# A decode kernel on one Trainium2 core: the last 64 rows of three weight matrices as two transfers each

## The chip, the core and the metric

The kernel runs on one core of one Trainium2 chip. TensorE (PE) multiplies matrices, VectorE (DVE), ScalarE (ACT) and GpSimd (POOL) do the rest, and SyncE (SP) issues nearly all loads, in one queue. A load is carried out by the core's 16 DMA engines. The metric is device time in microseconds of one launch.

## The reference

Two rounds of attention over a cache and a gated FFN, for four tokens (one per sequence) of 448 values:

```python
def _A_ref(x, k_cache, v_cache, wq, wo):          # 16 query heads, 8 KV heads of 256
    W = min(4096, max(256, Sk // 4))              # the last 2048 of 8192 positions
    q = (x @ wq).reshape(B, Sq, Hq, Dh) ...
    scores = jnp.einsum("bhqd,bhkd->bhqk", q, k) * (Dh ** -0.5)
    p = _softmax(scores, axis=-1)
    o = jnp.einsum("bhqk,bhkd->bhqd", p, v)
    return o ... @ wo

def _B_ref(x, w_gate, w_up, w_down):              # 448 -> 1792 -> 448
    return (_silu(x @ w_gate) * (x @ w_up)) @ w_down

x = x + _A_ref(_layernorm(x), ...)
x = x + _B_ref(_layernorm(x), ...)
x = x + _A_ref(_layernorm(x), ...)
x = x + _B_ref(_layernorm(x), ...)
return x
```

wq is 448 x 4096, gate and up are 448 x 1792, all bfloat16. Both rounds use the same weights and the same cache.

## The kernel before

The program is written as a graph of operations (`Graph.op`, and `Graph.dma` for loads). The order on each engine is written out by hand in the lists `SEQ_PE`, `SEQ_DVE`, `SEQ_ACT`, `SEQ_POOL` and `SEQ_SP`; `schedule` follows them and `_place_waits` puts semaphore waits only where an order does not give them already. So an engine never takes a later operation ahead of one that waits.

The cache goes through 27 buffers of 512 KB (`half`), and seven more that hold wq until the first queries have been made. `SLOTS` names the buffer of each load. A K load is 1 MB (L837) or 512 KB (L843), a V load 512 KB (L859). Each waits on SP, where it must, for the TensorE work that last used its buffer, and everything behind it in the SP queue waits too. VectorE transposes the K halves in place (L849); TensorE makes the scores (L883), transposes them (L930) and multiplies with V (L961); the results go through wo (L1014, L1006).

Weights are loaded once, by `load` (L487). With 448 = 3 x 128 + 64 rows, wq, gate and up come as three chunks of 128 rows and a tail of 64 rows. A tail is laid over all 128 partitions: the left half of its columns in partitions 0 to 63, the right half in partitions 64 to 127. In the source's access pattern the first dimension is the half (2), then the row (64), then the column:

```python
load(1 << 19, wq_sb[:, 3 * 4096:], A_wq[384:448, :].rearrange("r (h c) -> h r c", h=2), "wq3", 4096)
```

TensorE uses the tail of wq in `qproj` (L581, with `xe` as the small operand), those of gate and up in `ffn` (L706) and `ffn_row` (L643). In the SP queue the wq tail is the eighth load, behind three K loads, x and the three other chunks of wq. Between it and the tail of up stand seventeen loads, between that and the tail of gate nine; the large parts of gate, up and down come last of the weights.

The list `SEQ_PE` also has matrix products that compute nothing (L1093, "fillers": a zero operand is added to bank A); they stand at fixed places in the order.

Of the kernel before, what the change touches and what calls it, by code (L numbers as in the profile page):

```python
# [17 lines left out]
FF = 1792  # L18
# [140 lines left out]
class Op:  # L159
# [3 lines left out]
    def __init__(self, i, eng, kind, emit):  # L163
        self.i, self.eng, self.kind, self.emit = i, eng, kind, emit
        self.deps = {}
        self.nbytes = 0
        self.dsem = None
        self.dval = 0
        self.cells = self.rel = self.bank = ()
        self.inc = False  # L170
        self.val = 0
        self.waits = []


class Graph:
# [14 lines left out]
    def op(self, eng, kind, emit, r=(), w=(), bank=(), acc=()):  # L190
        o = Op(len(self.ops), eng, kind, emit)
        o.bank, o.tag = bank, self.tag
        self.ops.append(o)
        for k in r:
            d = self.writer.get(k)
            if d is not None:
                self._dep(o, d, d.eng != eng or eng != PE)
        for k in tuple(w) + tuple(acc):
            for d in self.readers.get(k, ()):
                self._dep(o, d, d.eng != eng or eng != PE)  # L200
            d = self.writer.get(k)
            if d is not None:
                self._dep(o, d, d.eng != eng or eng != PE)
        if eng != PE and "A" in bank:
            self._dep(o, self.last_a, self.last_a is not None and (self.last_a.eng != eng or eng != PE))
            self.last_a = o
        for b in bank:
            owner, now, before = self.banks.get(b, (eng, [], []))
            if owner != eng:
                owner, now, before = eng, [], now  # L210
            for d in before:
                self._dep(o, d, True)
            self.banks[b] = (owner, now + [o], before)
        for k in r:
            self.readers.setdefault(k, []).append(o)
        for k in tuple(w) + tuple(acc):
            self.writer[k] = o
            self.readers[k] = []
        return o

    def dma(self, nbytes, emit, sem, r=(), w=(), cells=(), run=4096):
        o = self.op(SP, "ld", emit, r=r, w=w)
        o.nbytes, o.cells, o.run = nbytes, cells, run
        if not cells:
            self._count(o, sem)
        return o

    def _count(self, o, sem):
        o.dsem = sem
        self.dcount[sem] = self.dcount.get(sem, 0) + 16  # L230
        o.dval = self.dcount[sem]

    def schedule(self, filler):
# [82 lines left out]
    def emit(self, eng_name, eng, sems, dsems):  # L316
        for o in self.order[eng_name]:
            for d in o.waits:
                if d.dsem is not None:
                    eng.wait_ge(dsems[d.dsem], d.dval)  # L320
                else:
                    eng.wait_ge(sems[d.eng], d.val)
            ins = o.emit(eng)
            if o.dsem is not None:
                ins.then_inc(dsems[o.dsem], 16)
            elif o.inc:
                ins.then_inc(sems[eng_name], 1)

# [10 lines left out]
def build(nc, A_x, A_k_cache, A_v_cache, A_wq, A_wo, B_x, B_w_gate, B_w_up, B_w_down, out):  # L339
    s0 = A_k_cache.shape[2] - WIN  # L340
    g = Graph()

    with ExitStack() as es:
# [8 lines left out]
        wq_sb = kv[:, NPOOL * HALF:]  # L352
# [75 lines left out]
        for a in range(4):  # L428
            g.op(DVE, "d1", lambda e, a=a: e.memset(qmask[32 * a:32 * a + 32, a:a + 1], DH ** -0.25), r=("qmask",),
                 w=(f"qmask{a}",))  # L430
# [10 lines left out]
        for P in range(2):  # L441
            g.op(DVE, "d1", lambda e, P=P: e.tensor_reduce(
                nmask[:, 2 * P:2 * P + 2], idq[:, P, :, 0:4, :].rearrange("p h a n -> p n h a"), AX.XY, ALU.add),
                r=("identb",), w=("rs0",))
        g.op(DVE, "d1", lambda e: e.tensor_reduce(negm[0][:, 0:1], nmask[:, :], AX.X, ALU.add), r=("rs0",), w=("negm0",))
        g.op(DVE, "d1", lambda e: e.tensor_scalar(negm[0][:, 1:2], negm[0][:, 0:1], -2.0, 1.0, op0=ALU.mult, op1=ALU.add),
             r=("negm0",), w=("negm0",))
# [10 lines left out]
        for h in range(2):  # L458
            for y in range(2):
                g.op(DVE, "d1", lambda e, h=h, y=y: e.tensor_copy(sel1[h][:, :, :, y, :], ivq[:, :, h:4:2, :]),  # L460
                     r=("identb",), w=(f"sel1{h}{y}",))
# [10 lines left out]
        for P in range(2):  # L472
            g.op(DVE, "d1", lambda e, P=P: e.tensor_reduce(
                osel[:, 2 * P:2 * P + 2], iv[:, :, 0, P, :, :].rearrange("p j y n -> p n j y"), AX.XY, ALU.max, negate=True),
                r=("identb",), w=("osel",))
        il = identb[:, :].rearrange("p (k y n) -> p k y n", y=2, n=2)
        g.op(DVE, "d1", lambda e: e.tensor_reduce(lomask[:, :], il[:, :, 1, :], AX.XY, ALU.add), r=("identb",),
             w=("lomask",))
# [3 lines left out]
        nw = [0]  # L482

        def load(nbytes, dst, src, key, run):
            nw[0] += 1
            g.tag = ("w", nw[0])
            g.dma(nbytes, lambda e: e.dma_start(dst, src), f"w{nw[0]}", w=key if isinstance(key, tuple) else (key,), run=run)  # L487
            g.tag = None

        load(4000, xio[0:B, :], A_x[:, 0, :], xio_k, 896)  # L490
        for cc in range(3):
            load(1 << 20, wq_sb[:, 4096 * cc:4096 * (cc + 1)], A_wq[128 * cc:128 * cc + 128, :], f"wq{cc}", 8192)
        load(1 << 19, wq_sb[:, 3 * 4096:], A_wq[384:448, :].rearrange("r (h c) -> h r c", h=2), "wq3", 4096)
        wo_v = A_wo.rearrange("(k p) n -> p k n", p=128)

        def load_wo(kvh):
# [3 lines left out]
        def load_ffn():  # L500
            for nm, wsb, src in (("wg", wg_sb, B_w_gate), ("wu", wu_sb, B_w_up)):
                load(3 * 458752, wsb[:, 0:3 * FF].rearrange("p (c n) -> p c n", c=3),
                     src[0:384, :].rearrange("(c p) n -> p c n", p=128), nm + "a", 3584)
                load(229376, wsb[:, 3 * FF:], src[384:448, :].rearrange("r (h c) -> h r c", h=2), nm + "b", 1792)
            load(1605632, wd_sb[:, :, :], B_w_down.rearrange("(c p) n -> p c n", p=128), "wd", 896)


# [283 lines left out]
        def x_in(e):  # L791
            clear(e, Zb[0:64, 12:16], 4)
            for cc in range(4):
# [6 lines left out]
             r=("z",), w=tuple(f"xs{t}" for t in range(B)) + tuple(f"x{t}" for t in range(B)), bank=("Z",))  # L800
# [197 lines left out]
        def out_proj(oi, ts, kvh, column):  # L998
# [21 lines left out]
            else:  # L1020
                g.op(PE, "opr", row, r=ro, acc=tuple(f"row{t}" for t in ts), bank=("A",))

        load_ffn()
        g.tag = None
        used = [None, None]
        gi, oc, waiting, wo_in = 0, 0, [], []
        for si, (heads, splits) in enumerate(zip(plan(), plan_splits())):
            where = {}
            for batch, split in zip(heads, splits):
                members, outs = [], []  # L1030
                for m in batch:
# [3 lines left out]
                    if kvh not in where:  # L1035
                        ts = sorted(t_ for b in heads for t_, _, k_ in b if k_ == kvh)
                        where[kvh] = (oc % 2, ts)
                        if used[oc % 2] != ts:
# [3 lines left out]
                                 w=tuple(f"oT{oc % 2}_{t_}" for t_ in range(B)))  # L1042
# [56 lines left out]
        dsems = {d: es.enter_context(nc.semaphore(f"d_{d}")) for d in g.dcount}  # L1099
# [28 lines left out]
def bass_interleave_layers__sliding_block_cached__swiglu_ffn__decode_kernel(  # L1128
    nc, A_x, A_k_cache, A_v_cache, A_wq, A_wo, B_x, B_w_gate, B_w_up, B_w_down, out
):  # L1130
    build(nc, A_x, A_k_cache, A_v_cache, A_wq, A_wo, B_x, B_w_gate, B_w_up, B_w_down, out)
# [28 lines left out]
```

## Time and profile before

| | |
|---|---|
| median of 3 runs | 313.45 us (311.82 to 316.13) |
| the profiled execution | 311.48 us, of which span 309.5 us |
| busy share: PE, DVE, ACT, POOL | 81%, 62%, 20%, 26% |
| loaded from HBM | 103.91 MB, 336 GB/s over the span |
| chain that ended last, by engine | PE 38%, DMA 23%, DVE 17%, SP's queue 15% |

The profile is of one execution. Times in its rows are from the start of the span. A row of the timeline gives start, duration, engine, line, operation, tiles and count, and in brackets how long the engine had been idle and what ended that. "SPq" is the SP queue issuing a load: its duration is how long the queue stood on that issue, not how long the load took. A row of the list of issues gives the load, the count, the size and the median time from issue to landing, in us. A row of the waits gives who waited for whom, the total in us, how often, and the longest.

### The profile page before, as it was taken

How to read it: one execution, taken by the hardware profiler on the slowest of the kernel's cores; microseconds unless marked ns; L12 is line 12 of the kernel's file. 1: busy time of each engine (PE TensorE's matmuls, PEld its weight loads, DVE VectorE, ACT ScalarE, POOL GpSimd, SP SyncE). 2: the span in 40 equal slices, each digit the busy share in tenths (PEclk: the TensorE clock that was granted, in tenths of full speed). 3: DMA queues.
4: the chain of work that ended last, by engine and by line, in shares of the span. 5: the costliest groups of instructions: out<-in, count | busy, mean ns of one | idle time of the engine just before them, and what ended most of it. 6: DMA issues, size and time to landing. Idle time of an engine off the chain costs nothing.

```text
span 309.5 us, 10634 instructions
## 1 busy us (share of the span) xinstructions
PE 249.5 (81%) x4683; PEld 140.9 (46%) x4683; DVE 193.2 (62%) x571; ACT 62.7 (20%) x173; POOL 80.3 (26%) x225
## 2 busy tenths in 40 slices
PE   4870478994759998778989788897999789989886
PEld 1320133431315754444545444363475437666565
DVE  4680085415235227886795959879479878768851
ACT  0001001010011132222223213223322332042311
POOL 0060012100201223404141442324223333233241
PEclk9977599998679999989999999999999999997997
DMA  7999995396999979999999999999999997999600
GB/s 295 428 313 280 358 411 238 142 327 251 315 399 364 318 267 329 420 411 412 330 346 411 411 413 413 411 381 340 374 420 412 408 407 284 367 421 406 277 2 5
DMA packets 26851, 104.60 MB, mean 338 GB/s; under 512 B 2609, under 2 KB 6709, under 8 KB 22837
## 3 DMA queue, kind: packets, MB, share of 16 engines
q1 hardware_dynamic: 26797, 103.92, 88.1%
q8 instruction: 37, 0.61, 0.8%
q14 instruction: 9, 0.07, 0.1%
q10 hardware_dynamic: 8, 0.00, 0.0%
HBM read 103.91 MB, written 0.00 MB: 336 GB/s over the span
## 4 chain that ended last, share of the span: by engine, by line
PE 38%; DMA 23%; DVE 17%; SPq 15%; issue 3%; ACT 3%; POOL 1%; DVEq 0%; ACTq 0%
DMA half<-in_A_v_cache_dram 14%; SPq L859 10%; PE A L1093 9%; DVE half L849 9%; PE S L883 6%; PE Y L961 6%; DMA half<-in_A_k_cache_dram 4%; DMA wo_sb<-in_A_wo_dram 4%; SPq L837 3%; PE A L1006 2%; PE Z L706 2%; PE A L1014 2%; DVE po L978 2%; SPq L487 2%; PE Y L930 2%
## 5 line engine op out<-in xcount | busy, mean ns | idle before, releaser
L849 DVE STREAM_TRANSPOSE half<-half 128x1024 uint32<-128x1024 uint32 x88 | 107.0, 1229 | 27.4 <-DMA half<-in_A_k_cache_dram 27.2
L1093 PE MATMUL A<-identb,small 128*128 128x512 bf16 x270 | 82.6, 403 | 5.0 <-DVE A L420 4.5
L961 PE MATMUL Y<-half,pT 128*8 128x256 bf16 (+1 forms) x1024 | 45.7, 280 | 9.8 <-DMA half<-in_A_v_cache_dram 7.1
L974 POOL TENSOR_TENSOR small<-small 128x2 f32<-128x2 f32 (+1 forms) x48 | 38.6, 807 | 36.8 <-DVE small L952 33.7
L883 PE MATMUL S<-half,qe 128*8 128x128 bf16 (+1 forms) x1536 | 44.7, 245 | 2.5 <-POOL qe L889 1.2
L1093 PEld LDWEIGHTS A<-identb,small 128*128 128x128 bf16 x270 | 24.2, 104 | 31.4 <-issue 14.6
L889 POOL TENSOR_TENSOR qe<-qc,tiny 128x64 bf16<-128x64 bf16 x64 | 18.1, 294 | 76.0 <-PE S L883 35.4
L883 PEld LDWEIGHTS S<-half,qe 128*8 128x8 bf16 x1536 | 31.2, 86 | 12.3 <-POOL qe L889 2.7
L978 DVE SCALAR_TENSOR_TENSOR po<-po,small,Y 128x256 bf16<-128x256 bf16 x48 | 22.6, 471 | 17.7 <-ACT po L976 17.4
L917 ACT ACTIVATE po<-S,small 104x128 bf16<-104x128 f32 (+1 forms) x48 | 19.3, 402 | 70.5 <-DVE small L913 70.3
L961 PEld LDWEIGHTS Y<-half,pT 128*8 128x8 bf16 (+1 forms) x1024 | 19.6, 84 | 23.2 <-DMA half<-in_A_v_cache_dram 8.6
L976 ACT ACTIVATE po<-Y 128x256 bf16<-128x256 f32 x48 | 18.4, 383 | 50.1 <-PE Y L961 33.2
L939 ACT ACTIVATE pT<-Y 128x64 bf16<-128x64 f32 (+1 forms) x48 | 12.4, 259 | 50.1 <-PE Y L930 48.4
L899 DVE TENSOR_REDUCE tiny<-S 104x1 bf16<-104x128 f32 (+1 forms) x48 | 15.3, 324 | 10.8 <-PE S L883 10.4
L1014 PE MATMUL A<-wo_sb,oT 128*4 128x448 bf16 x184 | 16.9, 370 | 5.7 <-DMA wo_sb<-in_A_wo_dram 3.7
L543 POOL TENSOR_SCALAR st<-st 128x1 f32<-128x1 f32 x16 | 4.3, 269 | 63.9 <-DVE st L535 52.4
L1041 POOL MEMSET oT<- 128x16 bf16 x38 | 4.2, 112 | 41.9 <-PE A L1014 34.6
L581 PE MATMUL Z<-half,xe 128*4 128x512 bf16 x40 | 4.1, 399 | 11.9 <-DMA half<-in_A_wq_dram 11.3
L913 DVE TENSOR_REDUCE small<-S 104x1 f32<-104x32 f32 x48 | 8.7, 182 | 7.2 <-PE S L907 6.1
L904 PE MATMUL S<-small,identb 104*104 104x32 bf16 x48 | 9.8, 212 | 3.6 <-DVE tiny L899 2.5
L952 DVE TENSOR_REDUCE small<-Y 128x2 f32<-128x32 f32 (+1 forms) x48 | 9.0, 190 | 6.0 <-PE Y L947 5.8
L994 DVE TENSOR_TENSOR oT<-Y,small 128x4 bf16<-128x4 f32 (+1 forms) x63 | 8.9, 154 | 5.0 <-PE Y L984 1.8
(130 smaller groups left out, 267.5 us busy)
## 6 DMA issues: line engine op xcount, KB each, us to landing
half<-in_A_v_cache_dram SPq DMA_DIRECT2D x87, 512.0 KB, 10.1
half<-in_A_k_cache_dram SPq DMA_DIRECT2D x28, 1024.0 KB, 10.0
half<-in_A_k_cache_dram SPq DMA_DIRECT2D x32, 512.0 KB, 7.2
wo_sb<-in_A_wo_dram SPq DMA_DIRECT2D x8, 448.0 KB, 13.4
half<-in_A_wq_dram SPq DMA_DIRECT2D x3, 1024.0 KB, 12.4
wd_sb<-in_B_w_down_dram SPq DMA_DIRECT2D x1, 1568.0 KB, 20.3
wg_sb<-in_B_w_gate_dram SPq DMA_DIRECT2D x1, 1344.0 KB, 15.7
wu_sb<-in_B_w_up_dram SPq DMA_DIRECT2D x1, 1344.0 KB, 18.2
```

The costliest lines, as they stand in the source:

```text
L849: return e.transpose(a, a)
L859: g.dma(1 << 19, lambda e, cell=cell, hv=hv, vsrc=vsrc: e.dma_start(unit(cell), vsrc[hv]), None, w=(f"v{t}_{kvh}_{hv}",), cells=(cell,))
L883: last = e.matmul(Sb[s_][qd:qd + 8, 0:32 * 2 * J], lhsT=qe[q_][:, P, ce, :, :].rearrange("p a n -> p (a n)"), rhs=keys(kcs[P], J * x, J, c ...
L889: g.op(POOL, "qe", lambda e, P=P, t=t, kvh=kvh: e.tensor_tensor(qe[q_][:, P, :, :, :], qc[t][:, kvh, :, :].unsqueeze(2).broadcast_to([128, ...
L899: g.op(DVE, f"max{n}", lambda e: e.tensor_reduce(pmax[s_][0:R, :], Sb[s_][0:R, 0:N], AX.X, ALU.max), r=(f"s{s_}",), w=(f"pmax{s_}",), bank ...
L917: return e.activation(praw[0:R, 0:128 * n].rearrange("p (g r l) -> p g r l", g=2 * n, l=2), Sb[s_][0:R, 0:128 * n].rearrange("p (l g r) -> ...
L961: last = e.matmul(Yb[p_][32 * gg:32 * gg + M, 256:512], lhsT=pT[pt][:, gg, 2 * a + hv, 4 * P:4 * P + M] if n == 2 else p1[:, gg % 2, 2 * a ...
L974: g.op(POOL, f"pow{n}", lambda e: e.tensor_tensor(ri[p_][:, 0:2 * n], rs[p_][:, 0:2 * n], expo[:, 1:1 + 2 * n], op=ALU.pow), r=(f"rs{p_}", ...
L976: g.op(SCA, "oh", lambda e: e.activation(oh[:, :], Yb[p_][:, 256:512], ACT.Copy), r=(f"y{p_}",), w=("oh",), bank=(f"Y{p_}",))
L978: g.op(DVE, "oho", lambda e: e.scalar_tensor_tensor(out=oh[:, :], in0=oh[:, :], scalar=lomask[:, 0:1], in1=Yb[p_][:, 256:512], op0=ALU.mul ...
L1014: last = e.matmul(Ab[32 * k:32 * k + B, 0:D], lhsT=oT[oi][:, k % 2, k // 2, :], rhs=wo_sb[:, 4 * kvh + k, :], start=False, stop=False, ski ...
L1093: return e.matmul(Ab[:, 0:512], lhsT=zero[:, 0:1].broadcast_to([128, 128]), rhs=identb[:, :].unsqueeze(1).broadcast_to([128, 4, 128]), sta ...
```

## The change

The tail's source is given as two column halves of 64 rows each, and `load` issues one transfer for each, into partitions 0 to 63 and 64 to 127. Both count on the same semaphore, so it is complete at 32 instead of 16 (`parts=2`). All else, the order of each engine included, stays.

```diff
-    def dma(self, nbytes, emit, sem, r=(), w=(), cells=(), run=4096):
+    def dma(self, nbytes, emit, sem, r=(), w=(), cells=(), run=4096, parts=1):
         o = self.op(SP, "ld", emit, r=r, w=w)
         o.nbytes, o.cells, o.run = nbytes, cells, run
         if not cells:
-            self._count(o, sem)
+            self._count(o, sem, parts)
         return o
 
-    def _count(self, o, sem):
+    def _count(self, o, sem, parts=1):
         o.dsem = sem
-        self.dcount[sem] = self.dcount.get(sem, 0) + 16
+        self.dcount[sem] = self.dcount.get(sem, 0) + 16 * parts
         o.dval = self.dcount[sem]
...
             if o.dsem is not None:
-                ins.then_inc(dsems[o.dsem], 16)
+                for i in ins if isinstance(ins, list) else (ins,):
+                    i.then_inc(dsems[o.dsem], 16)
...
         def load(nbytes, dst, src, key, run):
             nw[0] += 1
             g.tag = ("w", nw[0])
-            g.dma(nbytes, lambda e: e.dma_start(dst, src), f"w{nw[0]}", w=key if isinstance(key, tuple) else (key,), run=run)
+            if isinstance(src, tuple):
+                g.dma(nbytes, lambda e: [e.dma_start(dst[64 * h:64 * h + 64], src[h]) for h in range(2)], f"w{nw[0]}",
+                      w=(key,), run=run, parts=2)
+            else:
+                g.dma(nbytes, lambda e: e.dma_start(dst, src), f"w{nw[0]}", w=key if isinstance(key, tuple) else (key,),
+                      run=run)
             g.tag = None
+
+        def halves(src, n):
+            return src[384:448, 0:n], src[384:448, n:2 * n]
...
-        load(1 << 19, wq_sb[:, 3 * 4096:], A_wq[384:448, :].rearrange("r (h c) -> h r c", h=2), "wq3", 4096)
+        load(1 << 19, wq_sb[:, 3 * 4096:], halves(A_wq, 2048), "wq3", 4096)
...
-                load(229376, wsb[:, 3 * FF:], src[384:448, :].rearrange("r (h c) -> h r c", h=2), nm + "b", 1792)
+                load(229376, wsb[:, 3 * FF:], halves(src, 896), nm + "b", 1792)
```

## The prediction

> **What bounds the kernel now.** I read the slices first, for where the transfers run below their best, then the transfer queue in order of time, then the waits of TensorE and VectorE, then the chain of waits. The slices of the span (one is 7.74 us):
>
> ```profile
> PEclk9977599998679999989999999999999999997997
> ...
> GB/s 295 428 313 280 358 411 238 142 327 251 315 399 364 318 267 329 420 411 412 330 346 411 411 413 413 411 381 340 374 420 412 408 407 284 367 421 406 277 2 5
> ```
>
> From slice 16 on the rate is often 406 to 421 GB/s; the first fourteen lie between 142 and 428 and average 317, although the same kinds of loads are issued throughout. The granted clock dips in slices 2 to 4 and 9 to 11. At 411 GB/s a 512 KB load (524288 bytes) takes 1.28 us and a 224 KB load (229376 bytes) 0.56 us. The list of issues gives size and time to landing:
>
> ```profile
> half<-in_A_wq_dram SPq DMA_DIRECT2D x3, 1024.0 KB, 12.4
> ...
> half<-in_A_wq_dram SPq DMA_DIRECT2D x1, 512.0 KB
> wu_sb<-in_B_w_up_dram SPq DMA_DIRECT2D x1, 224.0 KB
> wg_sb<-in_B_w_gate_dram SPq DMA_DIRECT2D x1, 224.0 KB
> ```
>
> The three tails that the change touches have no landing time here, so each is measured by the loads before and after it. The SP queue's timeline, where the second number is how long the queue stood on the issue:
>
> ```profile
> 2.44 2.35 SPq L487 DMA_DIRECT2D half<-in_A_wq_dram  x4
> 4.83 9.99 SPq L859 DMA_DIRECT2D half<-in_A_v_cache_dram  x1
> ...
> 43.59 2.32 SPq L859 DMA_DIRECT2D half<-in_A_v_cache_dram  x1
> 45.95 1.75 SPq L487 DMA_DIRECT2D wu_sb<-in_B_w_up_dram  x1
> 47.74 10.71 SPq L859 DMA_DIRECT2D half<-in_A_v_cache_dram  x1
> ...
> 68.64 0.97 SPq L487 DMA_DIRECT2D wo_sb<-in_A_wo_dram  x1
> 69.65 1.02 SPq L487 DMA_DIRECT2D wg_sb<-in_B_w_gate_dram  x1
> 70.71 5.62 SPq L859 DMA_DIRECT2D half<-in_A_v_cache_dram  x1
> ```
>
> The third 1 MB piece of wq, just ahead of the wq tail, is issued at 3.64 by the chain of waits:
>
> ```profile
> 3.64 0.45 SPq L487
> ```
>
> Times to landing of single issues, in order of issue: the load ahead of the wq tail and the one behind it, the same for the up tail, the same for the gate tail:
>
> ```profile
> half<-in_A_wq_dram SPq DMA_DIRECT2D x1, 1024.0 KB, 15.2
> half<-in_A_v_cache_dram SPq DMA_DIRECT2D x1, 512.0 KB, 30.9
> half<-in_A_v_cache_dram SPq DMA_DIRECT2D x1, 512.0 KB, 18.6
> half<-in_A_v_cache_dram SPq DMA_DIRECT2D x1, 512.0 KB, 21.2
> wo_sb<-in_A_wo_dram SPq DMA_DIRECT2D x1, 448.0 KB, 11.5
> half<-in_A_v_cache_dram SPq DMA_DIRECT2D x1, 512.0 KB, 16.6
> ```
>
> So landings are 3.64 + 15.2 = 18.8 and 4.83 + 30.9 = 35.7 around the wq tail, 62.2 and 68.9 around the up tail, 80.1 and 87.3 around the gate tail. Less the 1.28 us of the later load itself, the tails held the queue's last lane for 15.6, 5.4 and 5.9 us: 26.9 us for 960 KB (983040 bytes), 37 GB/s, where the later slices move 411. This is the rate of about one or two of sixteen equal lanes (2/16 of 411 is 51). I infer that a tail sits on very few DMA engines, and that each later load, which is spread over all of them, is complete only when its share behind the tail has passed. What waits for that, by the timeline of TensorE and VectorE:
>
> ```profile
> 20.50 3.00 PE L1093 MATMUL A<-identb,small 128*128 128x512 bf16 x12
> 34.83 0.60 PE L581 MATMUL Z<-half,xe 128*4 128x512 bf16 x4 [11.32 <-DMA half<-in_A_wq_dram]
> 35.36 3.02 PE L1093 MATMUL A<-identb,small 128*128 128x512 bf16 x7
> ...
> 57.29 4.49 PE L1093 MATMUL A<-identb,small 128*128 128x512 bf16 x20
> ...
> 78.71 0.59 PE L961 MATMUL Y<-half,pT 128*4 128x256 bf16 x8 [5.78 <-DMA half<-in_A_v_cache_dram]
> ...
> 88.61 0.36 PE L1014 MATMUL A<-wo_sb,oT 128*4 128x448 bf16 x4 [3.69 <-DMA wo_sb<-in_A_wo_dram]
> ...
> 90.50 1.46 PE L1093 MATMUL A<-identb,small 128*128 128x512 bf16 x3
> ```
>
> ```profile
> 38.30 3.50 DVE L849 STREAM_TRANSPOSE half<-half 128x1024 uint32<-128x1024 uint32 x3 [15.28 <-DMA half<-in_A_k_cache_dram]
> ```
>
> TensorE stands 11.32 + 5.78 + 3.69 = 20.8 us behind late loads before 89 us. Between 89.1 and 155 us the waits for loads are small (total, times, longest):
>
> ```profile
> PEld Y L961 <- DMA half<-in_A_v_cache_dram: 1.8, 3, 0.9
> ...
> DVE half L849 <- DMA half<-in_A_k_cache_dram: 1.8, 4, 0.7
> ...
> PE Y L961 <- DMA half<-in_A_v_cache_dram: 1.2, 3, 0.6
> ```
>
> There the order on the engines sets the pace. The first 89 us are bound by transfers that are late because of the tails.
>
> **The change, part by part.**
>
> *Removed.* Three transfers that hold the queue's last lane 26.9 us. If the halves spread as the other loads do, the same bytes take 983040 / 411 GB/s = 2.4 us. The transfer side gains 26.9 - 2.4 = 24.5 us by the time the gate tail has passed.
>
> No row shows a load into 64 partitions. The cheap end is 2.4 us, the row rate of 411; the dear end is the rate of the tails now, 26.9 us and no gain. I take the cheap end, since the loads into 128 partitions that go at 411 are nearest in row length (4 KB, as the wq tail) and differ only in how many partitions they reach; 4.8 us, half that rate, is within my range.
>
> [...]
>
> *Added.* One more issue for each tail. An issue of wq stands 0.45 us on the queue (the row at 3.64), the longest issue ahead of the gate tail 0.97. Three such are 1.4 to 2.9 us of queue time. It is hidden: at each of the three places the queue already stands 5.6 to 10.7 us on the next issue, and what is issued there lands 16 to 31 us later (the rows of 16.6, 21.2 and 30.9). If that cover were gone it would cost those 1.4 to 2.9 us. Each tail's semaphore is waited for at 32 instead of 16; no wait is added, and the order of all engines is the same.
>
> *The TensorE side.* The wq tail would land about 18.8 + 1.3 = 20.1 (21.4 at half rate). TensorE gets to it after its twelve fillers, at 20.50 + 3.00 = 23.5. So the 11.32 us vanish, and next are the K loads for VectorE at 38.30, which the shorter tail moves by 15.6 - 1.3 = 14.3 us, to 24.0: also in time. From there on both sides run some 11 to 14 us earlier. The 5.78 us (a V load that was behind the up tail) go because loads behind that tail are early by 14.3 + 5.4 - 0.6 = 19.1, against 11.3 to 14 of TensorE: 5 to 8 us more, about what the wait was. The 3.69 us (a wo load behind the gate tail) go because loads behind it are early by 24.5 against 17.1 plus the clock's share. Sum of the waits: 20.8 us.
>
> The granted clock adds to it (the two dips). Seven fillers at 35.36 take 3.02 us (0.43 each) and three at 90.50 take 1.46 (0.49 each), where twenty at 57.29 take 4.49 (0.22 each); the slow ones stand right behind long idle times. At 0.22 the seven would take 1.6 and the three 0.7, which is 2.2 us; with some more for the work at 79 us, 2 to 4 us. So TensorE could be early by 20.8 to 25, and the loads by 22 to 24.5 (with and without the half rate). The later of the two sides decides: **20.8 to 24.5**, and I take 23, since the clock is likely to come back at least in part where no idle time is left.
>
> *What keeps it.* The next loads that the work meets closely are those of gate, up and down. Up:
>
> ```profile
> 84.42 1.86 SPq L487 DMA_DIRECT2D wu_sb<-in_B_w_up_dram  x1
> ```
>
> ```profile
> wu_sb<-in_B_w_up_dram SPq DMA_DIRECT2D x1, 1344.0 KB, 18.2
> ```
>
> ```profile
> 104.45 1.46 PE L706 MATMUL Z<-xn,wu_sb 128*128 128x32 bf16 x42
> ```
>
> It lands at 102.6 and is used at 104.45, 1.8 us of room; it moves with the loads (22 to 24.5), the use with TensorE, so at most 1 us of a wait can come. Then the queue waits for work to free buffers:
>
> ```profile
> 103.77 1.15 SPq L843 DMA_DIRECT2D half<-in_A_k_cache_dram  x1
> 111.59 0.33 SPq L859 DMA_DIRECT2D half<-in_A_v_cache_dram  x1
> ```
>
> Between 104.9 and 111.59 nothing is issued; the loads after it are tied to TensorE's progress. From here on the whole pattern, its later waits for loads too, moves as it is.
>
> **The rivals.**
>
> *Only the first wait pays (0.12).* Past 40 us TensorE's rows run nearly without gaps, fillers included, so new waits for freed buffers or for VectorE's transposes could take the place of the 5.78 and 3.69. Speaks for it: the load at 47.74 stands 10.71 us on a buffer or the queue. Against: TensorE idles those 9.5 us for the very loads that come early. Then 11.3 to 14.3 us are gained: 297.2 to 300.2 on the profiled run's clock.
>
> *No change (0.05).* The two halves go one behind the other at the tails' rate of now, because a half is no wider on the engines than the whole was: 26.9 us of the last lane stay, and the time is 311.5, with the added issues uncovered 312.9 to 314.4. For it: the profile has no 64-row load that is faster. Against it: 37 GB/s is a tenth of what wide loads reach, so a half that is wide at all is faster. [...]
>
> *Slower (0.03).* Each half gets a single lane, both the same one. The tails' lane then carries twice the bytes: 26.9 us more, 311.5 + 26.9 = 338. It decides from the point where a half holds the lane longer than half of what the whole did. Nothing in the profile shows 64-row transfers on one lane.
>
> **How the numbers follow.** The profiled execution took 311.48 us, 309.5 of them span (the 2.0 around it stay); the median of three is 313.45 (311.82 to 316.13), so it is a quick one by 2 us. From it, 311.5 - 23 = 288.5; from the median, 290.5. I predict 289.5. The forecast (0.80) by its own bounds runs from 311.5 - 24.5 = 287.0 to 313.45 - 20.8 = 292.7. More of the clock, and spread of runs, could bring 283; the first rival reaches 300. A range from 283 to 299 leaves out the last two cases and a little of the first. A measurement of this kernel tells about 2% (6.3 us) from no change: faster 0.92, the forecast and the first rival; within 0.05; slower 0.03.
>
> **What would show it.** After the change the tails should have landing times of their own in the issue list, some 1 to 3 us behind the load ahead of them; the V issue behind the wq tail should stand well under 9.99 us, and land near 22 instead of 35.7. The slices before 90 us should show near 400 GB/s where work frees buffers in time. TensorE's wait at L581 should be gone and the waits at L961 and L1014 gone or under 1 us, the clock row without its dip in slices 9 to 11, and the gap in the issues before the FFN's end should stand some 23 us earlier. I am wrong if the tails' neighbours still land 5 to 16 us apart, or if those waits go and waits of TensorE for VectorE grow by as much.

## The result, and the profile after

The changed kernel takes 295.46 us (median of 4 runs, 291.07 to 296.49); the kernel before, run beside it, 313.23 (4 runs, 311.82 to 316.13). The ratio of the times is 0.9341, with a 95% interval of 0.9189 to 0.9493. The profiled execution took 294.8 us, 292.7 of them span, against 311.48 and 309.5: 16.7 us less. Run again later, the changed kernel took 292.65 (ratio 0.9327, 0.9276 to 0.9377). Medians and ranges take in every run, ratios only the runs that were not in a slower state of the chip (here 294.8 and 291.07 us of the changed kernel), so a ratio is not the quotient of the two medians.

The slices of the span after, one of 7.32 us, for the granted clock and the rate of the transfers:

```profile
PEclk9998999998999999998979999999999999997957
...
GB/s 285 428 298 416 411 412 362 383 340 394 405 392 363 303 381 422 415 403 370 366 345 370 400 417 411 379 332 390 357 414 419 407 401 305 392 421 408 176 2 3
```

The two troughs that the rates had before (142 to 327 GB/s in slices 6 to 10, counted from 0, and 280 in slice 3) are gone. Of the clock's dips in slices 2 to 4 (7, 7 and 5 tenths) and 9 to 11 (8, 6 and 7) a single 8 is left at each place. The same in stretches, where a row gives the stretch, its length, the busy time and count of TensorE, its weight loads, VectorE, ScalarE and GpSimd, the granted clock, the DMA share and GB/s. Before:

```profile
20.00:40.00 20.00, 8.68 (x53) 2.81 (x45) 4.64 (x8) 2.06 (x3) 2.90 (x9) 0.72 1.02 315
40.00:64.00 24.00, 20.59 (x279) 9.57 (x279) 13.39 (x29) 3.07 (x8) 4.57 (x12) 1.00 0.67 258
64.00:92.00 28.00, 18.34 (x187) 6.94 (x189) 9.06 (x21) 2.33 (x7) 1.87 (x4) 0.83 0.91 323
```

After:

```profile
20.00:40.00 20.00, 16.88 (x169) 7.24 (x170) 12.45 (x29) 4.16 (x7) 6.32 (x19) 0.91 1.02 401
40.00:64.00 24.00, 21.37 (x227) 8.79 (x224) 11.67 (x19) 1.73 (x5) 1.87 (x5) 1.00 1.03 372
64.00:92.00 28.00, 25.94 (x475) 15.57 (x475) 11.04 (x42) 3.85 (x12) 4.43 (x10) 0.94 1.04 393
```

In the first stretch TensorE did almost twice the work, and 401 GB/s came in where 315 did. The DMA share, the time that the packets took over sixteen engines' time, was 1.02 in both, so it does not tell how many bytes come in. The transfer queue in order of time (start, time on the issue); in the new kernel L489 issues the halves, L492 other weights, L868 the V loads:

```profile
2.45 1.49 SPq L492 DMA_DIRECT2D half<-in_A_wq_dram  x3
3.98 1.20 SPq L489 DMA_DIRECT2D half<-in_A_wq_dram  x2
5.22 0.58 SPq L868 DMA_DIRECT2D half<-in_A_v_cache_dram  x1
...
37.22 1.52 SPq L868 DMA_DIRECT2D half<-in_A_v_cache_dram  x1
...
55.91 0.58 SPq L868 DMA_DIRECT2D half<-in_A_v_cache_dram  x1
...
92.72 0.33 SPq L868 DMA_DIRECT2D half<-in_A_v_cache_dram  x1
```

The V loads at 5.22, 37.22 and 55.91 are the first behind the wq, up and gate tails. Behind the wq tail the queue now stands 0.58 us on the issue instead of 9.99. The chain of waits has the issue ahead of it, the third 1 MB piece of wq (start, time on the issue, what):

```profile
3.47 0.47 SPq L492
```

Its time to landing, the last figure, and those of the three V loads in their order:

```profile
half<-in_A_wq_dram SPq DMA_DIRECT2D x1, 1024.0 KB, 17.1
half<-in_A_v_cache_dram SPq DMA_DIRECT2D x1, 512.0 KB, 18.4
half<-in_A_v_cache_dram SPq DMA_DIRECT2D x1, 512.0 KB, 16.3
half<-in_A_v_cache_dram SPq DMA_DIRECT2D x1, 512.0 KB, 11.9
```

Issue plus time to landing gives 20.6 for the wq piece and 23.7 (by the unrounded times), 53.5 and 67.8 for the V loads. Before they were 18.8, 35.7, 68.9 and 87.3. The halves' own landing times are now listed (256 KB, 16.5 and 18.0 us); the last half of wq is in at 4.60 + 18.0 = 22.6.

TensorE where its three waits for loads were (start, busy time, line, operation, count, idle time before it in brackets):

```profile
20.67 1.42 PE L590 MATMUL Z<-half,xn 128*4 128x512 bf16 x12 [1.39 <-issue]
22.02 3.80 PE L1102 MATMUL A<-identb,small 128*128 128x512 bf16 x12
25.75 0.39 PE L590 MATMUL Z<-half,xe 128*4 128x512 bf16 x4
...
64.28 0.39 PE L970 MATMUL Y<-half,pT 128*4 128x256 bf16 x8 [2.71 <-DMA half<-in_A_v_cache_dram]
...
70.36 0.36 PE L1023 MATMUL A<-wo_sb,oT 128*4 128x448 bf16 x4
...
83.58 1.48 PE L715 MATMUL Z<-xn,wg_sb 128*128 128x32 bf16 x42 [0.33 <-DVE xn L542]
```

The 11.32 us ahead of the wq tail's products and the 3.69 us for wo are gone; of the 5.78 us for a V load 2.71 stay. The last row is the first product with gate, past the stretch that the tails disturbed. Its row before, on the same operands:

```profile
102.44 1.48 PE L706 MATMUL Z<-xn,wg_sb 128*128 128x32 bf16 x42 [0.33 <-DVE xn L533]
```

At this point the work is 18.9 us early. This product's start and the landings of the three V loads are the marks by which I compare all kernels below.

### The profile page after: what moved, and what is told of

It is laid out like the page before. It is cut to its first block, busy times and chain, and to the rows that moved or that the text cites. A ratio compares the mean times of both kernels' runs of the same rounds, so it can differ in the third digit from the quotient of the medians.

```text
span 292.7 us, 10637 instructions
## 1 busy us (share of the span) xinstructions
PE 250.8 (86%) x4683; PEld 142.6 (49%) x4683; DVE 193.3 (66%) x571; ACT 62.8 (21%) x173; POOL 80.4 (27%) x225
## 4 chain that ended last, share of the span: by engine, by line
PE 45%; DMA 23%; DVE 17%; SPq 8%; issue 3%; ACT 2%; POOL 2%; DVEq 0%; ACTq 0%
DMA half<-in_A_v_cache_dram 23%; PE S L892 10%; PE A L1102 9%; DVE half L858 8%; PE Y L970 6%; SPq L868 4%; PE A L1015 3%; SPq L846 3%; PE Z L715 2%; PE Z L590 2%; PE Z L752 2%; PE Z L779 2%; PE Y L939 2%; PE A L1023 2%; DVE po L987 2%
## 5 line engine op out<-in xcount | busy, mean ns | idle before, releaser
L892 PE MATMUL S<-half,qe 128*8 128x128 bf16 (+1 forms) x1536 | 45.7, 247 | 2.4 <-POOL qe L898 1.2
L1102 PEld LDWEIGHTS A<-identb,small 128*128 128x128 bf16 x270 | 24.4, 104 | 30.3 <-issue 13.3
L892 PEld LDWEIGHTS S<-half,qe 128*8 128x8 bf16 x1536 | 31.8, 87 | 12.2 <-POOL qe L898 2.7
L987 DVE SCALAR_TENSOR_TENSOR po<-po,small,Y 128x256 bf16<-128x256 bf16 x48 | 22.6, 471 | 16.0 <-ACT po L985 15.5
L985 ACT ACTIVATE po<-Y 128x256 bf16<-128x256 f32 x48 | 18.4, 382 | 48.1 <-PE Y L970 32.0
L552 POOL TENSOR_SCALAR st<-st 128x1 f32<-128x1 f32 x16 | 4.3, 269 | 67.1 <-DVE st L544 55.6
L993 PE MATMUL Y<-tiny,po 128*128 128x2 bf16 (+1 forms) x96 | 9.6, 169 | 2.7 <-DVE po L987 2.6
L993 PEld LDWEIGHTS Y<-tiny,po 128*128 128x128 bf16 x96 | 6.6, 99 | 10.6 <-DVE po L987 5.1
## 6 DMA issues: line engine op xcount, KB each, us to landing
wd_sb<-in_B_w_down_dram SPq DMA_DIRECT2D x1, 1568.0 KB, 20.6
```

The source lines that it names most:

```text
L892: last = e.matmul(Sb[s_][qd:qd + 8, 0:32 * 2 * J], lhsT=qe[q_][:, P, ce, :, :].rearrange("p a n -> p (a n)"), rhs=keys(kcs[P], J * x, J, c ...
L985: g.op(SCA, "oh", lambda e: e.activation(oh[:, :], Yb[p_][:, 256:512], ACT.Copy), r=(f"y{p_}",), w=("oh",), bank=(f"Y{p_}",))
L987: g.op(DVE, "oho", lambda e: e.scalar_tensor_tensor(out=oh[:, :], in0=oh[:, :], scalar=lomask[:, 0:1], in1=Yb[p_][:, 256:512], op0=ALU.mul ...
L993: last = e.matmul(Yb[p_][:, 2 * n * dh:2 * n * dh + 2 * n], lhsT=oh[:, :].rearrange("p (m e) -> p e m", e=2)[:, dh, :], rhs=osel[:, 0:2 * ...
L1102: return e.matmul(Ab[:, 0:512], lhsT=zero[:, 0:1].broadcast_to([128, 128]), rhs=identb[:, :].unsqueeze(1).broadcast_to([128, 4, 128]), sta ...
```

## The experiments

Two theories stood after the result. **A:** a tail sat on two engines, and the halves are spread over all engines but still pay, because each reaches only half of the partitions. **B:** the halves cost nothing to speak of, and what is missing of the forecast went elsewhere (into two issues, into the clock, into waits of work for work). The diffs are against the changed kernel. The kernel before, timed beside them, took 313.68 us with e1 to e4, 313.92 with f1 to f4 and 314.83 with g1 and g2.

**One transfer over all partitions** (e1_wide).

```diff
-        load(1 << 19, wq_sb[:, 3 * 4096:], halves(A_wq, 2048), "wq3", 4096)
+        load(1 << 19, wq_sb[:, 3 * 4096:], A_wq[384:448, :].rearrange("r (h c) -> (r h) c", h=2), "wq3", 4096)
...
-                load(229376, wsb[:, 3 * FF:], halves(src, 896), nm + "b", 1792)
+                load(229376, wsb[:, 3 * FF:], src[384:448, :].rearrange("r (h c) -> (r h) c", h=2), nm + "b", 1792)
```

> Each tail is one transfer again, but its source is read as 128 consecutive runs (row, then half), so the first dimension is 128 on both sides; half h of row r lies in partition 2r+h, which the rest of the kernel does not follow (the tail's products are of other numbers, the work is the same). Theory A (what made the old tail slow is its first dimension of 2; what the two halves still cost above a wide load, about 5.5 us by the landings, is that each reaches only 64 partitions): the 9.99 us issue and the 11.32 us wait are gone, and the first V load lands near 18.8 + 1.3 + 1.3 = 21.4 us instead of 23.7 with the halves; the time is 3 to 5 us under the changed kernel's, 290 to 292. Rival B (making two transfers is what helped): one transfer is as slow as before, 311 to 316. Rival C (the 5.5 us are not the tails' but a late lane's): like the changed kernel, 293 to 297, V load at 23 to 24.

Measured: 288.46 us (287.71 to 290.98), ratio to before 0.9246 (0.9178 to 0.9313). The first V load behind each tail, its issue and its time to landing:

```profile
4.52 0.47 SPq L868 DMA_DIRECT2D half<-in_A_v_cache_dram  x1
...
33.34 3.35 SPq L868 DMA_DIRECT2D half<-in_A_v_cache_dram  x1
...
52.06 0.51 SPq L868 DMA_DIRECT2D half<-in_A_v_cache_dram  x1
```

```profile
half<-in_A_v_cache_dram SPq DMA_DIRECT2D x1, 512.0 KB, 16.8
half<-in_A_v_cache_dram SPq DMA_DIRECT2D x1, 512.0 KB, 16.8
half<-in_A_v_cache_dram SPq DMA_DIRECT2D x1, 512.0 KB, 11.2
```

They land at 21.3, 50.2 and 63.3, which is 2.4, 3.3 and 4.5 us before those of the changed kernel. TensorE:

```profile
23.71 0.39 PE L590 MATMUL Z<-half,xe 128*4 128x512 bf16 x4
...
60.24 0.39 PE L970 MATMUL Y<-half,pT 128*4 128x256 bf16 x8 [1.04 <-DMA half<-in_A_v_cache_dram]
...
78.06 1.48 PE L715 MATMUL Z<-xn,wg_sb 128*128 128x32 bf16 x42 [0.33 <-DVE xn L542]
```

The wait for the V load is 1.04 us instead of 2.71, and the gate product is 24.4 us earlier than before the change, 5.5 more than in the first execution with halves. So the halves do cost time, against B. One transfer differs from two in more than one way, though: in their number, and in which partitions each reaches.

**Two transfers of every other partition** (e2_evenodd), 64 rows each as in the change, from the same sources.

```diff
-                g.dma(nbytes, lambda e: [e.dma_start(dst[64 * h:64 * h + 64], src[h]) for h in range(2)], f"w{nw[0]}",
+                g.dma(nbytes, lambda e: [e.dma_start(dst[h:128:2], src[h]) for h in range(2)], f"w{nw[0]}",
```

> Two transfers of 64 rows as in the changed kernel, but half 0 goes to the even partitions and half 1 to the odd ones, so that each reaches the whole height of the buffer (the products of the tail are of other numbers). Theory A with the reach of the destination as the cause of the rest: as with one wide transfer, first V load at about 21.4, 290 to 292. Rival D (the rest is a price of 64-row transfers, few rows for each engine, or of the strided source): as the changed kernel, V load near 23.7, 293 to 297.

Measured: 288.5 us (286.49 to 294.84), ratio 0.9211 (0.9145 to 0.9278). The first V load behind the wq tail, issued and landed:

```profile
5.31 0.58 SPq L868 DMA_DIRECT2D half<-in_A_v_cache_dram  x1
```

```profile
half<-in_A_v_cache_dram SPq DMA_DIRECT2D x1, 512.0 KB, 16.1
```

It lands at 21.4, the other two at 50.2 and 63.3, and the gate product starts at 77.94: all as with one wide transfer. Two transfers, 64 rows in each and a strided source are therefore not what costs (288.5 us against 288.46). What is left is that a half lies in 64 neighbouring partitions: behind such halves the V load of the gate tail landed at 67.8, behind halves in every other partition at 63.3. By what means the place of the partitions makes this difference is not shown.

**Quarters** (e3_quarters): four transfers of 32 rows into 32 partitions each.

```diff
-                g.dma(nbytes, lambda e: [e.dma_start(dst[64 * h:64 * h + 64], src[h]) for h in range(2)], f"w{nw[0]}",
-                      w=(key,), run=run, parts=2)
+                g.dma(nbytes, lambda e: [e.dma_start(dst[32 * i:32 * i + 32], src[i // 2][32 * (i % 2):32 * (i % 2) + 32]) for i in range(4)], f"w{nw[0]}",
+                      w=(key,), run=run, parts=4)
```

> Each tail as four transfers of 32 rows instead of two of 64. If the rest of 5.5 us is paid once for each transfer, it doubles: V load near 23.7 + 3 = 26.7, and 4 to 6 us over the changed kernel, 298 to 302. If it comes from how much of the height is reached at a time, and a quarter reaches no less than a half: V load near 23.7 and 293 to 298. If a quarter reaches half as much as a half: V load 25 to 27, 297 to 301.

Measured: 292.88 us (291.17 to 293.19), ratio 0.9362 (0.9309 to 0.9414). The V loads land at 23.3, 52.8 and 67.1, the gate product starts at 82.58. Quarters are as the halves are: neither the two added issues nor the shorter transfers show in the time. The changed kernel was not run beside the wide transfer, but the quarters were, and their quickest run (291.17) is slower than the slowest with the wide transfer (290.98).

**Halves from ScalarE's queue** (e4_act): the tails leave SyncE's queue; wq's is issued at the start, those of up and gate ahead of ScalarE's third operation.

```diff
+            for at, dst, src, sem in self.beside if eng_name == SCA else ():
+                if at == n:
+                    for h in range(2):
+                        eng.dma_start(dst[64 * h:64 * h + 64], src[h]).then_inc(dsems[sem], 16)
...
-                g.dma(nbytes, lambda e: [e.dma_start(dst[64 * h:64 * h + 64], src[h]) for h in range(2)], f"w{nw[0]}",
+                g.beside.append((0 if key == "wq3" else 2, dst, src, f"w{nw[0]}"))
+                g.dma(nbytes, lambda e: [], f"w{nw[0]}",
```

> The halves of the changed kernel, but issued from ScalarE: those of wq at its start, those of gate and up after its second operation (about 30 us), so that they run beside the wide loads of the SP queue and not ahead of them in it. Theory A with the reach as cause: beside wide loads the narrow ones cost little more than their bytes, so the landings behind get 3 to 5 us earlier: 289 to 293. Rival E (a narrow transfer costs its time wherever it runs): 293 to 297. A loss could come from ScalarE, which issues for some 1 us ahead of its first operation and 2 us behind its second, where its next operation is 7 us off: none expected.

Measured: 292.91 us (291.08 to 297.24), ratio 0.9355 (0.9277 to 0.9432). That is at the border of the two expectations, and level with the quarters (292.88), which ran beside it. In the profiled execution, the longest of the four with 297.24 us, the V loads land at 23.1 behind wq's place and 66.3 behind gate's. Another queue for the issues takes little off the landings, and no gain shows in the time.

**wq's tail alone, gate's and up's alone** (f1_wq_only, f2_gu_only): the other tails keep the form of before.

```diff
-                load(229376, wsb[:, 3 * FF:], halves(src, 896), nm + "b", 1792)
+                load(229376, wsb[:, 3 * FF:], src[384:448, :].rearrange("r (h c) -> h r c", h=2), nm + "b", 1792)
```

> Only the tail of wq comes as two transfers; up and gate are as before. Theory A: the shift of about 11.3 to 12 us that the changed kernel has at 57 us appears in full, and the waits behind the up and gate tails come back (5.8 and 3.7 us before), so the time is 311.5 - 11.5 = 300, between 298 and 303. Rival (the three tails share one cause, and a late lane alone keeps everything late): little gain, 306 to 313.

```diff
-        load(1 << 19, wq_sb[:, 3 * 4096:], halves(A_wq, 2048), "wq3", 4096)
+        load(1 << 19, wq_sb[:, 3 * 4096:], A_wq[384:448, :].rearrange("r (h c) -> h r c", h=2), "wq3", 4096)
```

> Only the tails of up and gate come as two transfers; wq is as before. Theory A: the 9.99 us issue and the 11.32 us wait stay, the waits of 5.8 and 3.7 us behind the other two tails shrink: 311.5 - 7 = 304.5, between 302 and 307. Rival (after the wq tail the work itself is the bound): 309 to 313.

Measured: 303.65 us (300.2 to 306.69), ratio 0.9638 (0.9559 to 0.9718) for wq alone; 305.32 (303.36 to 309.17), ratio 0.9693 (0.9623 to 0.9763) for gate and up alone. In the first, two of TensorE's waits of before (5.78 and 3.69 us) come back nearly whole (total, times, longest):

```profile
PE Y L970 <- DMA half<-in_A_v_cache_dram: 5.0, 2, 4.8
...
PE A L1023 <- DMA wo_sb<-in_A_wo_dram: 3.3, 1, 3.3
```

In the second, the first wait does (11.32 before):

```profile
34.70 0.59 PE L590 MATMUL Z<-half,xe 128*4 128x512 bf16 x4 [10.60 <-DMA half<-in_A_wq_dram]
```

By the ratios wq alone gains 3.6%, gate and up together 3.1%, in sum 6.7%; all three together gain 6.7% as well (0.9327, the changed kernel run beside them, below). So wq's tail and the pair of gate's and up's each pay for themselves; gate and up were not parted. The rival by which only the first wait pays is out: with wq alone the kernel stays 303.65 - 292.65 = 11.0 us slower than with all three.

**Two transfers of all partitions, each on the old form** (f3_cols): the tail is split by columns, and each part keeps the source that begins with the dimension of two.

```diff
-                g.dma(nbytes, lambda e: [e.dma_start(dst[64 * h:64 * h + 64], src[h]) for h in range(2)], f"w{nw[0]}",
+                n = src[0]
+                g.dma(nbytes, lambda e: [e.dma_start(dst[:, c * n:c * n + n], src[1][:, :, c * n:c * n + n]) for c in range(2)], f"w{nw[0]}",
...
-            return src[384:448, 0:n], src[384:448, n:2 * n]
+            return n // 2, src[384:448, :].rearrange("r (h c) -> h r c", h=2)
```

> Each tail comes as two transfers too, but each of all 128 partitions and half the columns, with the old source pattern (half, row, column) in each. Theory A: the first dimension is still 2, so the landings lag as before, and the time is that of before, 311 to 317 (the same bytes in runs half as long). Rival B (two transfers instead of one are what helps): as the changed kernel, 293 to 297.

Measured: 308.73 us (308.14 to 311.03), ratio 0.985 (0.9793 to 0.9908). It is nowhere near the halves, so two transfers as such don't do it. But it is under the 311 to 317 that I expected of theory A. The queue stands 10.92 us on the two issues, as it stood 9.99 on the V load behind the tail before, and the V load goes out late:

```profile
3.96 10.92 SPq L490 DMA_DIRECT2D half<-in_A_wq_dram  x2
14.92 5.04 SPq L869 DMA_DIRECT2D half<-in_A_v_cache_dram  x1
```

```profile
half<-in_A_v_cache_dram SPq DMA_DIRECT2D x1, 512.0 KB, 17.4
```

It lands at 32.3, where it landed at 35.7 before. TensorE's first wait falls with it:

```profile
31.41 0.59 PE L591 MATMUL Z<-half,xe 128*4 128x512 bf16 x4 [7.53 <-DMA half<-in_A_wq_dram]
```

The traces also hold the times at which a transfer's semaphore is raised. One wide transfer has sixteen such events (e1_wide, wq: 19.0 to 20.1), which I read as one for each engine that is done. The events of the tails' semaphores (us):

```
                wq                            up                       gate
before          3: 5.2, 33.3, 34.7            3: 48.1, 66.3, 67.9      3: 71.1, 84.5, 86.2
after           32: 19.2 to 22.6              32: 49.2 to 52.4         32: 63.3 to 66.6
f3_cols         6, the late ones 23.7, 23.9, 31.1, 31.3
```

A half has sixteen events, a tail of the old form two late ones (the first, at 5.2, 48.1 and 71.1, comes within 2.2 us of its issue). By that reading it sits on two engines, within the one or two lanes that the prediction read from 37 GB/s.

**The changed kernel again** (f4_after_again), beside these three, without an edit.

> The changed kernel again, beside the others on one chip: 291 to 297. First V load at 23 to 24 us, as in its first profile, if that is no accident of one execution; the half-rate stretch of TensorE's clock near the end (10 us at 277 us there) at another place or gone.

Measured: 292.65 us (291.52 to 294.06), ratio 0.9327 (0.9276 to 0.9377). The V loads land at 23.6, 53.0 and 67.1, the gate product starts at 81.65. The two executions of the changed kernel differ by up to 0.7 us in the landings, much less than the 3.8 to 4.5 us that part them from the wide transfer. At the gate product they differ by 1.9 us, so what the wide transfer gains there over the halves is 3.6 to 5.5 us, not 5.5 alone.

**Quarters in alternating order** (g1_alternating), partitions 0, 64, 32 and 96 in turn:

```diff
-                g.dma(nbytes, lambda e: [e.dma_start(dst[64 * h:64 * h + 64], src[h]) for h in range(2)], f"w{nw[0]}",
-                      w=(key,), run=run, parts=2)
+                g.dma(nbytes, lambda e: [e.dma_start(dst[32 * i:32 * i + 32], src[i // 2][32 * (i % 2):32 * (i % 2) + 32]) for i in (0, 2, 1, 3)], f"w{nw[0]}",
+                      w=(key,), run=run, parts=4)
```

> Each tail as four transfers of 32 rows as in the run with quarters, but in the order of partitions 0, 64, 32, 96, so that the two halves of the height take turns every 32 rows. Same result as with the quarters and the halves if the transfer side cannot overlap even such short stretches: first V load at 23.3 to 23.7 us, ratio to before 0.930 to 0.938. If the short stretches overlap (the lanes are up to 2 us apart, a quarter of the wq tail is about 0.6 us at half rate): V load at 21.4 to 22.5, ratio 0.918 to 0.928.

Measured: 292.87 us (291.8 to 296.92), ratio 0.9297 (0.9234 to 0.9361). The V loads land at 23.0, 52.7 and 66.8, the gate product starts at 82.61. That is between the two expectations and in time no other than the plain quarters: neighbours in the queue that reach different partitions do not make up for each other here, or hardly (23.0 us against 23.3 at the first V load, 292.87 against 292.88 in time).

**A half in partitions 32 to 95** (g2_middle), the other half in two pieces around it, with the normalized input of those rows written to match.

```diff
-                g.dma(nbytes, lambda e: [e.dma_start(dst[64 * h:64 * h + 64], src[h]) for h in range(2)], f"w{nw[0]}",
-                      w=(key,), run=run, parts=2)
+                g.dma(nbytes, lambda e: [e.dma_start(dst[p:p + n], src[h][r:r + n]) for p, n, h, r in ((32, 64, 0, 0), (0, 32, 1, 0), (96, 32, 1, 32))], f"w{nw[0]}",
+                      w=(key,), run=run, parts=3)
...
-                vec(f"nx{1 + h}", lambda e, h=h: e.tensor_scalar(
-                    xe[64 * h:64 * h + 64, h, t:t + 1], x[64:128, t, 3:4], Z2[64:128, 0:1], None, op0=ALU.subtract),
+                vec(f"nx{1 + h}", lambda e, h=h: [e.tensor_scalar(
+                    xe[p:p + 32, h, t:t + 1], x[q:q + 32, t, 3:4], Z2[q:q + 32, 0:1], None, op0=ALU.subtract)
+                    for p, q in (((32, 64), (64, 96)), ((0, 64), (96, 96)))[h]][-1],
```

> A tail's left half goes in one transfer to partitions 32 to 95, its right half in two of 32 rows to 0 to 31 and 96 to 127; xe is filled to match, with two VectorE instructions more for each norm. If reaching only one half of the height is the cause, the first of the three goes at the full rate and only the other two pay: about half of the 5.5 us is won, V load at 22.3 to 22.6, less about 0.2 us for each norm, so ratio 0.922 to 0.932. If any 64 neighbouring partitions are as slow: V load at 23.5, ratio 0.932 to 0.940.

Measured: 294.62 us (292.44 to 297.6), ratio 0.9362 (0.9304 to 0.9421). The first V load:

```profile
5.84 0.45 SPq L869 DMA_DIRECT2D half<-in_A_v_cache_dram  x1
```

```profile
half<-in_A_v_cache_dram SPq DMA_DIRECT2D x1, 512.0 KB, 16.4
```

It lands at 22.2, the others at 51.4 and 64.8, 1.5 to 3.0 us ahead of the changed kernel's and 0.9 to 1.5 behind the wide transfer's. Where the half lies made the difference here, in halves of one size too. The time did not follow: the gate product starts at 80.59, and the kernel ends no earlier than the changed one. The waits for loads have nearly gone (total, times, longest):

```profile
DVE half L859 <- DMA half<-in_A_k_cache_dram: 0.4, 1, 0.4
...
PE Y L971 <- DMA half<-in_A_v_cache_dram: 0.2, 1, 0.2
```

In the changed kernel the same two groups were

```profile
DVE half L858 <- DMA half<-in_A_k_cache_dram: 9.6, 6, 2.8
...
PE Y L970 <- DMA half<-in_A_v_cache_dram: 3.8, 5, 2.7
```

So waits for loads no longer hold it up. The lead over the kernel before, 21.9 us at the gate product, is 15.1 at the end. Taken at the same operations of ScalarE, it falls from 22.6 to 14.8 between 142 and 224 us on the clock of before, and from 160 us of its own span on the granted clock was lower than in the changed kernel (a row as above, g2_middle first):

```profile
160.00:240.00 80.00, 69.99 (x1425) 38.86 (x1424) 60.68 (x164) 21.90 (x62) 26.18 (x75) 0.94 0.98 373
```

```profile
160.00:240.00 80.00, 69.69 (x1529) 40.34 (x1518) 62.22 (x165) 22.13 (x64) 26.19 (x75) 1.00 1.00 394
```

The clock is not shown to be the whole account: at a mean clock of 0.961 g2_middle took 292.44 us, and the changed kernel at 0.963 took 291.07. VectorE also has 32 instructions more (603 instead of 571). Whether these, or the way the order falls out later, cost part of the gain was not tried.

## Why the prediction was right, and which term was off

**The cause of the late loads, the few engines: right.** Two late completions for each old tail, sixteen for each half, and f3_cols, which keeps the old form in two transfers, keeps most of the loss (308.73 us against 292.65).

**The waits and the clock: right in direction, two of three in full.** The first wait and the wo wait went, and the dips of the clock shrank. The wq products stand at 25.75, not at 23.5, so 34.83 - 25.75 = 9.1 us were won instead of 11.32: the wq piece ahead of the tail landed at 20.6 instead of 18.8, TensorE began with it 1.5 us later (20.67 against 19.12), and its twelve fillers took 3.80 us instead of 3.00. With the wide transfer the products stand at 23.71. The V wait of 5.78, forecast as gone or under 1 us, kept 2.71 with halves and 1.04 with the wide transfer.

**The mis-sized term: "I take the cheap end".** The halves were put at the rate of wide loads, 2.4 us for all three tails. The transfer side should then have been early by 14.3, 19.1 and 24.5 us behind the wq, up and gate tails. It was early by:

```
first V load behind     wq      up      gate
forecast               14.3    19.1    24.5
changed kernel         12.0    15.4    19.5
e1_wide                14.4    18.8    24.0
```

The wide transfer gives the forecast's row to within 0.5 us: the sum was right for a load that reaches all partitions. The halves cost 4.5 us more than it (3.8 in f4_after_again), so 2.4 + 4.5 = 6.9 us in all, and 983040 bytes / 6.9 us = 142 GB/s, about a third of 411. Half rate, the 4.8 us that the prediction held within its range, is shown by no run: by the landings the halves took 6.2 to 6.9 us, and why is open. The work followed the loads: in the eleven traces of changed kernels the lead of the V load behind the gate tail (4.4 to 24.0 us) and that of the gate product (3.6 to 24.5) differ by at most 0.9 us. The changed kernel has 19.5 and 18.9, in f4_after_again 20.2 and 20.8.

**What keeps it: right up to the FFN's gap, in part behind it.** The first V issue behind the FFN's gap moved from 111.59 to 92.72, 18.9 us, the same as the gate product. At the same operations of ScalarE the lead then moves between 17.2 and 19.9 us, and is 18.5 at 296 us on the clock of before; the last 1.6 were lost at the end of the profiled execution. Two stretches that begin equally long before the end, before and after:

```profile
291.80:303.80 12.00, 10.92 (x258) 8.51 (x247) 5.82 (x32) 2.96 (x8) 5.33 (x14) 0.88 0.03 12
```

```profile
275.00:287.00 12.00, 11.28 (x214) 8.41 (x213) 4.63 (x28) 2.26 (x7) 4.81 (x13) 0.57 0.01 3
```

The granted clock is 0.57 instead of 0.88, and TensorE gets through 214 products instead of 258. f4_after_again shows such a dip at its end as well (0.57 from 279.8 to 291.8 us), but lost more of its lead earlier: 20.8 us at the gate product, 18.8 after a stretch at 0.52 from 186 to 193 us, 17.7 at the end. In e1_wide, 24.4 us early at the gate product, 23.9 are left at the end (spans of 309.5 and 285.6). What calls the dips up is not known from these runs.

**The sum.** Forecast 23. The halves take 23 - 18.9 = 4.1 of it, what was lost behind the gate product 18.9 - 16.9 = 2.0, which leaves the 16.9 us at the end (16.7 by the whole times). In f4_after_again the two are 2.2 and 3.1, which leaves 17.7. From median to median it was 313.23 - 295.46 = 17.8, and 21.3 when it ran again. The 295.46 lie outside the forecast's own bounds of 287.0 to 292.7, and inside the range of 283 to 299 only because that was drawn wide enough for other cases; the later 292.65 lie at the edge of those bounds.

**The rivals.** That only the first wait pays is refuted by f2_gu_only, whose other two tails gain 313.92 - 305.32 = 8.6 us. No change and slower are refuted by the result.

**Signs.** The queue's stand behind the wq tail (0.58), the tail's landing 2 us behind the load ahead of it, the rates and, but for a single 8, the clock row came as said; the V load was to land near 22 and landed at 23.7.

## What to carry to other kernels

Look at which dimension a transfer's source begins with (here a wq tail that begins with 2 had two late events, one that begins with 64 or 128 sixteen for each transfer), and read its cost from the loads ahead of it and behind it, since the tails on few engines did not show as low DMA use throughout (the share was 1.02 in the first stretch, 0.67 in the second) and had no landing time in their own rows: the V loads behind them landed late (35.7, 68.9 and 87.3 us, behind the wide tails 21.3, 50.2 and 63.3). Splitting the tails into halves won most of it back (the gate product started 18.9 to 20.8 us earlier), and a pattern that spreads over all partitions, in one transfer or in two interleaved ones, won the rest (24.4 and 24.5 us earlier). Whether the time follows depends on the later side of the two, so move both marks, the landing and the work that uses it, before adding up a gain.

The wide layouts of e1_wide and e2_evenodd put half h of row r into partition 2r + h. In these runs the products took the tail's rows as they lay, without an input laid out to match, so the 288.5 us is what the transfers allow and not a finished version. One with the input to match was not tried; g2_middle, which has such an input for its own layout, did not turn earlier loads into time.

## What the runs showed of the hardware that was not expected

- Halves in 64 neighbouring partitions cost 2.6 to 2.9 times what a wide transfer of the same bytes does, not twice (for the three tails 2.4 us at the 411 GB/s of the later slices, and 3.8 to 4.5 us more by the landings behind them, an estimate), and a half in partitions 32 to 95 with its rest around it cost less (V load at 64.8, between 63.3 and 67.1).
- The wide load just ahead of the halves was later too: the 1 MB piece of wq landed at 20.6 with halves behind it and at 18.8 with the old tail, though issued 0.2 us earlier (3.47 and 3.64).
- The time was the same from another queue: halves issued from ScalarE's queue gave 292.91 us, from SyncE's, not run beside them, 292.65 (ratios 0.9355 and 0.9327).
- Tails of the old form in column halves, with rows half as long, passed sooner than in one piece: the V load behind the wq tail landed at 32.3 instead of 35.7, and the kernel was 1.5% faster (0.9793 to 0.9908). This is not explained.
